# Behind the loop: the last dh stores and half of K's reload on GpSimd's queue, four repeats on VectorE, two row sums in neighbouring column groups

## The chip, the cores and the metric

The kernel runs on one core of a Trainium2 chip. A core has TensorE (PE, matrix multiplications, with a separate weight load, PEld), VectorE (DVE), ScalarE (ACT), GpSimd (POOL) and SyncE (SP), which work on their own instruction streams in order and wait for one another by semaphores. SP, ACT and POOL also issue DMAs, each on a queue of its own; all transfers are carried out by the core's 16 DMA engines. The metric is the device time of one execution in microseconds (us); lower is better.

## What is computed

The reference is the forward pass and all gradients of a gated mixture of two branches over a sequence u of L = 2048 positions with D = 448 channels:

```
g   = sigmoid((u * gate_w).sum(-1))
a   = causal_conv(u, K) + u * Dskip        # K[d, l]: sum over N = 256 modes of C * exp(dt*A*l) * dt*B, by FFT
b   = relu(u @ w1 + b1)**2 @ w2 + b2       # F = 1792
out = g * a + (1 - g) * b
return out and the gradients of u, A, B, C (real and imaginary), log_dt, Dskip, w1, b1, w2, b2, gate_w
```

Two of the outputs matter below. `out_9`, the gradient of Dskip, is the sum over all positions of g times grad_out times u. `out_14`, the gradient of gate_w, is the sum over all positions of ds times u, where ds is the gradient at the sigmoid's input.

## The kernel before

All activations lie as 128 partitions by 16 slots by 448 channels. The order of the work is written out by hand; every engine executes its instructions in program order.

1. A first stage computes the forward spectra of u and of g times grad_out (`fwd1`, `fwd2`: two steps of an FFT, with a store to a scratch tensor `gd` and a load between them), the gradient of K (`dk_d`), and tables of powers.
2. A loop over 14 groups of 32 channels (`token`, `PERIOD`) builds K by products of tables (`kgen`, `k_out`) and, one group behind, reduces the gradient of K to the modes (`turn_x`, `turn_y`, `back_z`, `back_p`, `back_s`). The dense branch runs between these steps (`D_`, `first_layer`, `second_layer`, `project`): at each "D" of PERIOD a few of its 127 steps are taken, and `done` counts them. `dh` (line 968) computes one block of the hidden gradient on VectorE. Its store to `dhT_d` is not issued at once: it is put on the list `behind`, which `release()` empties at each KO, just after that group's `k_out`.
3. Behind the loop (from line 1159) `release()` is called once more. `rows_in` loads 512 KB rows of the dense branch for the weight gradients, on GpSimd's queue. The weight gradients are cut into units (`units`: `turn` transposes a row, `mul_rows` multiplies, `turn_back` writes out) which `Fl(n)` places between the other work.
4. K is then reloaded from its scratch tensor `k_d` into `xs`, so that it stands as 16 slots of 128 positions: thirteen calls of `reload` and three of `fix` (lines 1273 to 1283), all of them on SP. Positions from 256 on are rounded by the reference's bf16 position index, so many rows of `xs` are copies of others: `again` makes them within SBUF, four on VectorE for partitions 64 to 127 and six on ScalarE for partitions 32 to 63. The skip weight is added to the first row on VectorE, and `fwd1` (line 1430) takes `xs` to K's spectrum, with `fwd2` and the products of spectra behind it. Between the reload and `fwd1` the last channel group's `turn_y`, `back_z`, `turn_x`, `back_p` and `back_s` run, and the first units.
5. The inverse transforms (`inv1`, `inv2`) give the forward output (loop at line 1519) and the gradient of u (loop at line 1570). Between the two loops stand the row sums for `out_9` and `out_14` (line 1563): for each, sixteen matmuls with one weight column, one for each slot, accumulate in one PSUM row, ScalarE copies the row and GpSimd's queue stores it.

The loop's last KO (group 13) comes behind its last "D". By the formula in line 1145 all 127 steps have been taken by then, so `done` equals `total` there. The list `behind` holds four dh stores at that point, blocks 3 to 6 of the last column block, 256 KB each.

Of the kernel before, what the change touches and what calls it, by code (L numbers as in the profile page):

```python
# [19 lines left out]
P = 128  # L20
L, D, N, F = 2048, 448, 256, 1792
LT = L // P
# [306 lines left out]
def kernel(ctx, tc, A_u, A_A_re, A_A_im, A_B_re, A_B_im, A_C_re, A_C_im, A_log_dt, A_Dskip,  # L329
# [3 lines left out]
    nc = tc.nc  # L333
    V, S, G_, T_ = nc.vector, nc.scalar, nc.gpsimd, nc.tensor
# [5 lines left out]
    def dscr(name, n, dt=bf16):  # L340
        return nc.dram_tensor(name, (n,), dt, kind="Internal")
# [5 lines left out]
    k_d = dscr("k_d", VROW * D)  # L347
# [4 lines left out]
    dhT_d = dscr("dhT_d", F * L)  # L352
# [5 lines left out]
    K = Ker(tc, pool, psum)  # L358
# [43 lines left out]
    o = 0  # L402
# [34 lines left out]
    g_b = const.tile([P, LT], bf16, name="g_b")  # L437
# [43 lines left out]
    ps = K.ps("X", [P, FT + 4], bf16)  # L481
# [58 lines left out]
    ps = K.ps("S", [P, 512])  # L540
# [149 lines left out]
    behind = []  # L690

    def release():

        while behind:
            behind.pop(0)()
# [171 lines left out]
    def later(f):  # L867
        lates.append(f)
        if len(lates) > LAG:
            lates.pop(0)()  # L870
# [81 lines left out]
    def second_layer():  # L952

        load_r(7)
        for lb in range(4):
            dblk = dbl[lb % 2].rearrange("p (a l) -> p a l", a=DT)
            for jp in range(HP):
                i = HP * lb + jp
                pss = [bank(), bank()]
                for k in range(2):  # L960
                    for dt in range(DT - 1):
                        T_.matmul(pss[k][:], lhsT=w2Tw[:, jp, dt, k], rhs=dblk[:, dt], start=(dt == 0), stop=False, skip_group_check=True)  # L962
                for k in range(2):
                    h = slice(64 * k, 64 * k + 64)
                    T_.matmul(pss[k][:], lhsT=w2Tw[h, jp, 3, k], rhs=dblk[h, 3], start=False, stop=True, tile_position=(64 * k, 0), skip_group_check=True)  # L965
                for k in range(2):
                    S.mul(hblk[:, 2 * jp + k], pss[k][:], 2.0)  # L967
                def dh(i=i, jp=jp, lb=lb):
                    hb = hblk[:, 2 * jp:2 * jp + 2]
                    V.tensor_tensor(out=hb.rearrange("p k l -> p (k l)"), in0=hb.rearrange("p k l -> p (k l)"), in1=rr[i % 8], op=ALU.mult)  # L970
                    behind.append(lambda: nc.sync.dma_start(pair_rows(dhT_d, jp, lb), hb))
                    if i + 8 < 4 * HP:
                        behind.append(lambda: load_r(i + 8, nc.sync))
                later(dh)
                yield
            if lb < 2:
                behind.append(lambda lb=lb: load_db(lb + 2, nc.sync))
            yield from project(lb, 1, w1T)
# [56 lines left out]
    for k, (x8, g, e, gr) in enumerate(ekeys):  # L1035
        T_.matmul(tiles[e][32 * gr:32 * gr + 32, 0:D], lhsT=ct["Ew"][:, 32 * k:32 * k + 32], rhs=hss[x8 // 2][:, g, x8 % 2, :], start=(k == first[e, gr]), stop=(k == last[e, gr]),
                  tile_position=(0, 32 * gr), skip_group_check=True)
    stA, stB = (K.t("st", [P, 4, D], bufs=2) for i in range(2))
    for e in range(6):
        st_ = (stA if e < 4 else stB)[:, e % 4]  # L1040
        if e == 5:
            st_ = st_[0:1]
# [97 lines left out]
    for c in range(1, NCH):  # L1140
        k = 0
# [15 lines left out]
                for g in range(NG):  # L1157
                    nc.sync.dma_start(flat(Gts[0][32 * g:32 * g + 32]), tl(G2, g))
    D_(total)
    release()  # L1160
    Gt = Gts[0]
    DB2 = KW[:, NA * D:].rearrange("p (t d) -> p t d", d=D)

# [85 lines left out]
    def Fl(n=1):  # L1249
        nonlocal nf  # L1250
        for _ in range(n):
            next(fill, None)
            nf += 1

    Fx = K.t("F17", [P, 8704])
    xs = Fx[:, 0:7168].rearrange("p (t d) -> p t d", d=D)
# [3 lines left out]
    xq = 0  # L1260

    def reload(p0, n, j, m, row, *dims):

        nonlocal xq
        xq += 1
        nc.sync.dma_start(xs[p0:p0 + n, j:j + m].rearrange("p m d -> p (m d)"), bass.AP(tensor=k_d, offset=row * D, ap=[[x * D, y] for x, y in dims] + [[1, m * D]]))

    def fix(p0, step, n, j, row, st_):

        nonlocal xq  # L1270
        xq += 1
        nc.sync.dma_start(xs[p0:p0 + step * (n - 1) + 1:step, j], bass.AP(tensor=k_d, offset=row * D, ap=[[st_ * D, n], [1, D]]))
    reload(64, 64, 0, 2, 32, (2, 4), (48, 16))
    reload(64, 64, 3, 1, 48 + 32, (2, 4), (48, 16))
    reload(32, 32, 0, 4, 8, (4, 2), (48, 16))
    reload(32, 32, 7, 1, 48 + 8, (4, 2), (48, 16))
    for j, m, row in ((0, 4, 0), (4, 4, 16), (8, 8, 24)):
# [3 lines left out]
    fix(79, 16, 4, 3, 34, 2)  # L1281
    fix(47, 16, 2, 7, 12, 20)
    fix(31, 1, 1, 15, 8, 1)

    def again(p0, cp, j, m, i, step=1, rep_=1):

        dst = xs[p0:(2 * p0), j:j + 1]
        src = xs[p0:2 * p0, i:i + 1]
        cp(run(dst[:, 0, 0:1], 0, [step * D, rep_], [D, m], [1, D]), run(src[:, 0, 0:1], 0, [0, rep_], [D if step == 1 else 0, m], [1, D]))
# [28 lines left out]
    again(64, V.tensor_copy, 5, 2, 1, 4, 3)  # L1318
    again(64, V.tensor_copy, 7, 1, 3, 4, 3)
    for j, m, i in ((8, 4, 0), (4, 2, 0), (6, 1, 1), (12, 2, 2), (14, 1, 1), (15, 1, 7)):  # L1320
        again(32, S.copy, j, m, i)
    got = {32: [0, 1, 2, 3, 0, 1, 1, 7, 0, 1, 2, 3, 2, 3, 1, 7], 64: [0, 1, 0, 3, 0, 1, 1, 3] + [0, 1, 1, 3] * 2}
    for p0, w in ((32, {0: 0, 8: 1, 4: 2, 12: 3, 16: 7}), (64, {0: 0, 8: 1, 16: 3})):
        assert [w[int(vp[p0, j]) - LT * p0] for j in JO] == got[p0]
# [92 lines left out]
    rc = K.t("rec", [P, RS])  # L1417
# [56 lines left out]
    for q in range(4):  # L1474
# [5 lines left out]
        if q == 1:  # L1480
# [4 lines left out]
            Uv = U[:, :, 0:D]  # L1485
# [23 lines left out]
    Fl(2)  # L1509

    dgt = rc[:, 0:256].rearrange("p (k m) -> p k m", k=2)
    row = rc[0:1, 512:512 + 2 * D].rearrange("p (k d) -> p k d", k=2)
    dg = const.tile([P, LT], fp32, name="dg")
    gp = const.tile([P, LT], bf16, name="gp")
    V.tensor_tensor(out=gp[:], in0=g_b[:], in1=omg_b[:], op=ALU.mult)
# [1 line left out]
    ds_b = const.tile([P, LT], bf16, name="ds_b")  # L1517
    ds32 = const.tile([P, LT], fp32, name="ds32")
    for q in range(4):
# [4 lines left out]
        for x in range(2):  # L1524
            pp = K.pair()
            K.inv2(hs, q, x, pp, [[(negI, brq[q][:, hp, x])] for hp in range(2)])
            for hp in range(2):
                t = 2 * q + x + 8 * hp
                ps = pp[hp][:, 0:D]
# [22 lines left out]
    GU = GU_[:, 0:7168].rearrange("p (t d) -> p t d", d=D)  # L1552
# [7 lines left out]
    pgs = (None for dt in range(2, 4) for _ in param_grads(dt))  # L1560
    hsn = load_hs(2, 0)
    Fl(4)
    for k, (lw, rw, o_) in enumerate(((g_b, GU, out_9), (ds_b, Uv, out_14))):
        ps = K.ps("N%d" % k, [P, 512])
        for t in range(LT):
            T_.matmul(ps[0:1, 0:D], lhsT=lw[:, t:t + 1], rhs=rw[:, t, :], start=(t == 0), stop=(t == LT - 1))  # L1566
        S.copy(row[:, k], ps[0:1, 0:D])
        G_.dma_start(o_.rearrange("(o d) -> o d", o=1), row[:, k])
    Fl(5)
    for q in range(4):  # L1570
        hs = hsn
# [3 lines left out]
        for x in range(2):  # L1575
            ps = K.pair()
            l0l = 2 * q + x
            for hp in range(2):
                t = l0l + 8 * hp
# [17 lines left out]
    ps = K.ps("N1", [P, P], bf16)  # L1597
# [6 lines left out]
    ps = K.ps("X", [P, P], bf16)  # L1604
# [34 lines left out]
```

## Time and profile before

| | us |
|---|---|
| median of three runs | 816.03 |
| lowest, highest | 811.8, 819.44 |
| the profiled execution's own time | 817.63 |
| its span, first to last instruction | 815.8 |

| engine | busy us | share of the span | instructions |
|---|---|---|---|
| PE | 621.9 | 76% | 6749 |
| PEld | 299.4 | 37% | 6749 |
| DVE | 625.3 | 77% | 983 |
| ACT | 506.0 | 62% | 831 |
| POOL | 163.9 | 20% | 264 |

The mean granted TensorE clock is 0.86 of full speed. A row of the profile names the line of the kernel (L1266), the engine (SPq and the like are the engine's own issuing of DMAs), the operation, and the tiles as "written<-read". A name in brackets with an arrow is what ended the idle time before it. Times in the timeline count from the span's start. DMA share is the mean busy share of the 16 DMA engines.

### The profile page before, as it was taken

The page shows a single profiled execution, that of the slowest core. Times are in us where ns is not written, and L with a number is a line of the kernel's source. Part 1 is how long each engine was busy: PE and PEld are TensorE (multiplying, and loading weights), DVE is VectorE, ACT ScalarE, POOL GpSimd, SP SyncE. Part 2 cuts the span into 40 slices and gives each one's busy share as a digit, 9 for nine tenths or more (in the row PEclk, how much of TensorE's full clock was granted, in tenths as well). Part 3 has the DMA queues.
Part 4 walks back from the last instruction along what each step waited for, and adds up shares of the span by engine and source line. Part 5 has one row for each costly group of instructions (what it writes and reads, how often), then busy time and mean ns, then how long its engine had stood idle before and what let it go on. Part 6 is the DMA issues. An engine that isn't in the chain of part 4 may idle for free. (4 is left out here: it accounts for less than half of the span.)

```text
span 815.8 us, 16878 instructions
## 1 busy us (share of the span) xinstructions
PE 621.9 (76%) x6749; PEld 299.4 (37%) x6749; DVE 625.3 (77%) x983; ACT 506.0 (62%) x831; POOL 163.9 (20%) x264
## 2 busy tenths in 40 slices
PE   3676467653378889898978978898778788899985
PEld 1222222121234344344534443444534333444442
DVE  3795597877826999999889999998656974687353
ACT  0696567670577676677866766673675577264553
POOL 1222000042111222222321011101034311023112
PEclk9965655575689999899989999999989799799998
DMA  9978866278758577978696979996689998899972
GB/s 193 237 200 279 302 244 231 90 291 208 209 115 180 114 179 167 174 157 191 190 187 119 288 190 251 181 263 162 212 311 324 343 314 282 260 281 330 261 196 64
DMA packets 179694, 178.87 MB, mean 219 GB/s; under 512 B 116549, under 2 KB 157471, under 8 KB 179023
## 3 DMA queue, kind: packets, MB, share of 16 engines
q1 hardware_dynamic: 152632, 101.04, 50.7%
q0 software_dynamic: 17552, 56.44, 22.6%
q10 hardware_dynamic: 9430, 20.31, 7.1%
q8 instruction: 53, 0.87, 0.4%
q14 instruction: 27, 0.21, 0.1%
HBM read 83.67 MB, written 67.53 MB: 185 GB/s over the span
## 5 line engine op out<-in xcount | busy, mean ns | idle before, releaser
L816 ACT CAST P<-psF 128x1024 bf16<-128x1024 f32 x56 | 57.0, 1018 | 36.5 <-PE psF L814 35.9
L656 DVE TENSOR_TENSOR F<-X,F 128x1024 bf16<-128x1024 bf16 (+2 forms) x42 | 64.4, 1533 | 4.1 <-ACT F L711 2.4
L882 PEld LDWEIGHTS <-U 128*128 128x128 bf16 x448 | 40.0, 100 | 52.9 <-issue 15.0
L882 PE MATMUL psN<-D,U 128*128 128x448 bf16 x224 | 52.6, 372 | 6.3 <-DMA D<-in_B_w_dram 3.6
L1196 PEld LDWEIGHTS <-S 128*128 128x128 bf16 x416 | 40.2, 101 | 40.9 <-issue 13.7
L887 POOL DMA_DIRECT2D br_d<-D x32 | 17.9, 560 | 182.7 <-ACT D L886 176.2
L814 PE MATMUL psF<-R,S 41*32 41x256 bf16 x896 | 24.4, 288 | 37.0 <-DVE P L827 16.8
L1196 PE MATMUL psX<-D,S 128*128 128x449 bf16 x224 | 49.4, 365 | 1.5 <-ACT S L1202 1.5
L882 PE MATMUL psN<-S,U 128*128 128x448 bf16 x224 | 48.0, 358 | 2.5 <-DVE U L970 2.4
L826 DVE TENSOR_TENSOR M<-P,psF 128x2048 bf16<-128x2048 bf16 x28 | 34.0, 1215 | 17.1 <-PE psF L772 17.1
L1196 PE MATMUL psX<-K,S 128*128 128x448 bf16 x192 | 43.7, 374 | 1.8 <-ACT S L1199 1.8
L962 PE MATMUL psN<-S,K 128*128 128x512 bf16 x168 | 44.4, 404 | 0.0
L1187 ACT ACTIVATE S<-psN 128x1024 bf16<-128x1024 bf16 x32 | 33.0, 1030 | 14.9 <-PE psN L1183 14.8
L904 PE MATMUL psN<-S,K 128*128 128x512 bf16 x168 | 42.2, 388 | 0.0
L967 ACT ACTIVATE U<-psN 128x512 bf16<-128x512 f32 x56 | 30.8, 605 | 15.5 <-PE psN L965 11.4
L303 PE MATMUL psN<-D,cb_MI 64*128 64x448 bf16 x96 | 31.7, 514 | 9.0 <-DVE D L288 5.7
L886 ACT CAST D<-psN 128x448 bf16<-128x448 f32 x32 | 17.0, 532 | 33.7 <-PE psN L882 33.7
L657 DVE TENSOR_TENSOR X<-F 128x512 bf16<-128x512 bf16 (+2 forms) x42 | 35.6, 849 | 1.4
L772 PE MATMUL psF<-ident,X 128*128 128x128 bf16 x448 | 33.1, 232 | 4.0 <-ACT P L816 3.9
L303 PEld LDWEIGHTS <-cb_MI 64*128 64x128 bf16 x256 | 17.0, 105 | 51.9 <-issue 46.5
L265 PEld LDWEIGHTS <-M 128*64 128x64 bf16 x192 | 13.8, 133 | 60.1 <-issue 53.6
L827 DVE TENSOR_TENSOR P<-P,psF 128x2048 bf16<-128x2048 bf16 x28 | 34.2, 1221 | 1.0
(346 smaller groups left out, 1596.6 us busy)
## 6 DMA issues: line engine op xcount, KB each, us to landing
sp<-K ACTq DMA_DIRECT2D x8, 896.0 KB
dhT_d<-U SPq DMA_DIRECT2D x28, 256.0 KB
R<-sp SPq DMA_DIRECT2D x8, 896.0 KB
S<-dhT_d POOLq DMA_DIRECT2D x14, 512.0 KB, 6.8
R<-hd SPq DMA_DIRECT2D x16, 448.0 KB
S<-rT_d POOLq DMA_DIRECT2D x12, 512.0 KB, 7.0
hd<-st SPq DMA_DIRECT2D x13, 448.0 KB
rec<-rec_d POOLq DMA_DIRECT2D x11, 448.0 KB, 4.6
```

Source lines behind the costliest of these rows:

```text
L303: nc.tensor.matmul(ps[kk2][:, 0:D], lhsT=MI[r0:r0 + 64, m, :], rhs=rh[r0:r0 + 64], start=(k_ == 0), stop=(k_ == len(terms) - 1), tile_posi ...
L656: V.tensor_tensor(out=Vt[:, 0:2 * w * n], in0=run(lo, 0, [0, 2], [NA, w], [1, n]), in1=run(PX[:, 0:1], 512 * k, [2, w], [0, n], [1, 2]), o ...
L657: V.tensor_tensor(out=run(lo, n, [NA * X2, 2], [NA, X2], [1, n]), in0=run(vb, 0, [n * X2, 2], [n, X2], [1, n]), in1=run(vb, (w + X2) * n, ...
L772: T_.transpose(ps[:, t, 128 * b:128 * b + 128], Xs[c % 2][:, o_:o_ + 128], ident[:])
L816: S.copy(zbs[c, g // 2][:, :, g % 2].rearrange("p t h k n -> p t k h n"), psz[:].rearrange("p t (k h n) -> p t k h n", k=2, h=2))
L826: V.tensor_tensor(out=pr.rearrange("p t g h k n -> p t (g h k n)"), in0=zv, in1=xv, op=ALU.mult)
L827: V.tensor_tensor(out=zv, in0=zv, in1=rev_dim(xv, 1), op=ALU.mult)
L882: T_.matmul(ps[:, 0:D], lhsT=hblk[:, j, P * tt:P * tt + P], rhs=ws[:, j, :], start=(w == 1 and j == 0), stop=(j == FT - 1))
L904: T_.matmul(pss[k][:], lhsT=w1w[:, dt, j * P:j * P + P], rhs=UT[:, dt, 512 * lb:512 * lb + 512], start=(dt == 0), stop=False, skip_group_c ...
L962: T_.matmul(pss[k][:], lhsT=w2Tw[:, jp, dt, k], rhs=dblk[:, dt], start=(dt == 0), stop=False, skip_group_check=True)
L1187: S.activation(hn(i)[:, 8 * th:8 * th + 8, :], ps[:], ACT.Square if i < FT else ACT.Copy)
L1196: T_.matmul(ps[:, 0:w], lhsT=hn(i)[:, t, :], rhs=(DB2[:, t, :] if i < FT else U[:, t, 0:w]), start=(t == 0), stop=(t == LT - 1))
```

## The change

- The dh stores take POOL's queue when all dense steps are done at the time they are issued, else SP's as before.
- The extra `release()` moves from ahead of the units to behind K's reload. (By the order above, the release in the last KO has emptied the list before either place.)
- The sixteen loads of K's reload alternate between POOL's and SP's queue, beginning with POOL: eight each.
- Of the six copies for partitions 32 to 63, the first two (four slots and two slots) stay on ScalarE; the other four (one, two, one and one slots) go to VectorE.
- The two row sums are interleaved slot by slot. They write rows 0 and 32 of one PSUM bank from column groups 0 and 32 of TensorE; the two copies and stores follow behind both.

```diff
-                    behind.append(lambda: nc.sync.dma_start(pair_rows(dhT_d, jp, lb), hb))
+                    behind.append(lambda: (G_ if done >= total else nc.sync).dma_start(pair_rows(dhT_d, jp, lb), hb))
...
     D_(total)
-    release()
     Gt = Gts[0]
...
     def reload(p0, n, j, m, row, *dims):
         nonlocal xq
         xq += 1
-        nc.sync.dma_start(xs[p0:p0 + n, j:j + m].rearrange("p m d -> p (m d)"), ...)
+        (nc.sync, G_)[xq % 2].dma_start(xs[p0:p0 + n, j:j + m].rearrange("p m d -> p (m d)"), ...)
     def fix(p0, step, n, j, row, st_):
         nonlocal xq
         xq += 1
-        nc.sync.dma_start(xs[p0:p0 + step * (n - 1) + 1:step, j], ...)
+        (nc.sync, G_)[xq % 2].dma_start(xs[p0:p0 + step * (n - 1) + 1:step, j], ...)
...
     fix(31, 1, 1, 15, 8, 1)
+    release()
...
     for j, m, i in ((8, 4, 0), (4, 2, 0), (6, 1, 1), (12, 2, 2), (14, 1, 1), (15, 1, 7)):
-        again(32, S.copy, j, m, i)
+        again(32, S.copy if j in (8, 4) else V.tensor_copy, j, m, i)
...
-    for k, (lw, rw, o_) in enumerate(((g_b, GU, out_9), (ds_b, Uv, out_14))):
-        ps = K.ps("N%d" % k, [P, 512])
-        for t in range(LT):
-            T_.matmul(ps[0:1, 0:D], lhsT=lw[:, t:t + 1], rhs=rw[:, t, :], start=(t == 0), stop=(t == LT - 1))
-        S.copy(row[:, k], ps[0:1, 0:D])
-        G_.dma_start(o_.rearrange("(o d) -> o d", o=1), row[:, k])
+    ps = K.ps("N0", [P, 512])
+    for t in range(LT):
+        for k, (lw, rw) in enumerate(((g_b, GU), (ds_b, Uv))):
+            T_.matmul(ps[32 * k:32 * k + 1, 0:D], lhsT=lw[:, t:t + 1], rhs=rw[:, t, :], start=(t == 0), stop=(t == LT - 1),
+                      tile_position=(0, 32 * k), skip_group_check=True)
+    for k, o_ in enumerate((out_9, out_14)):
+        S.copy(rc[32 * k:32 * k + 1, 512:512 + D], ps[32 * k:32 * k + 1, 0:D])
+        G_.dma_start(o_.rearrange("(o d) -> o d", o=1), rc[32 * k:32 * k + 1, 512:512 + D])
```

More of the change, by code (lines that the diff above doesn't have):

```diff
@@ L1265, in reload @@
         xq += 1
-        nc.sync.dma_start(xs[p0:p0 + n, j:j + m].rearrange("p m d -> p (m d)"), bass.AP(tensor=k_d, offset=row * D, ap=[[x * D, y] for x, y in dims] + [[1, m * D]]))
+        (nc.sync, G_)[xq % 2].dma_start(xs[p0:p0 + n, j:j + m].rearrange("p m d -> p (m d)"), bass.AP(tensor=k_d, offset=row * D, ap=[[x * D, y] for x, y in dims] + [[1, m * D]]))
     def fix(p0, step, n, j, row, st_):
@@ L1271, in fix @@
         xq += 1
-        nc.sync.dma_start(xs[p0:p0 + step * (n - 1) + 1:step, j], bass.AP(tensor=k_d, offset=row * D, ap=[[st_ * D, n], [1, D]]))
+        (nc.sync, G_)[xq % 2].dma_start(xs[p0:p0 + step * (n - 1) + 1:step, j], bass.AP(tensor=k_d, offset=row * D, ap=[[st_ * D, n], [1, D]]))
     reload(64, 64, 0, 2, 32, (2, 4), (48, 16))
@@ L1511 @@
     dgt = rc[:, 0:256].rearrange("p (k m) -> p k m", k=2)
-    row = rc[0:1, 512:512 + 2 * D].rearrange("p (k d) -> p k d", k=2)
     dg = const.tile([P, LT], fp32, name="dg")
```

## The prediction

> **What bounds the kernel now.** The change touches two places, the 30 us behind the loop (570 to 601 us of the span) and two row sums at 753 us. So I read the stretches around them first (time from:to, length, busy time of PE, weight loads, DVE, ACT, POOL with instructions, granted clock, DMA share, GB/s).
>
> ```profile
> 584.00:594.50 10.50, 6.15 (x69) 3.94 (x67) 5.26 (x8) 7.17 (x9) 0.00 (x0) 0.99 0.34 93
> 594.50:622.50 28.00, 25.32 (x161) 13.94 (x161) 20.84 (x48) 18.59 (x29) 13.88 (x24) 0.88 0.98 328
> 757.50:760.50 3.00, 3.00 (x17) 1.27 (x15) 0.00 (x0) 0.61 (x2) 0.49 (x2) 1.00 0.49 131
> 760.00:785.00 25.00, 22.17 (x173) 11.34 (x172) 11.17 (x28) 14.56 (x35) 6.54 (x12) 0.94 1.01 286
> 785.00:816.00 31.00, 20.34 (x157) 10.55 (x155) 14.25 (x39) 13.00 (x32) 5.73 (x11) 0.89 0.29 74
> ```
>
> From 584 to 594.5 neither PE (6.15 of 10.5 us) nor the DMA engines (0.34) are full: something else holds the kernel. From 594.5 on both are nearly full. Next, the orders of the two queues and who SP waited for in 569 to 625 us (total, times, longest):
>
> ```profile
> 570.39 0.90 SPq L763 DMA_DIRECT2D k_d<-P  x2
> 571.39 6.19 SPq L971 DMA_DIRECT2D dhT_d<-U  x4
> 578.40 12.28 SPq L1266 DMA_DIRECT2D F<-k_d  x13
> 590.72 1.66 SPq L1272 DMA_DIRECT2D F<-k_d  x3
> 592.50 0.35 SPq L383 DMA_DIRECT2D M<-c_M  x1
> ```
> ```profile
> SPq L255 <- DMA gd<-D: 5.5, 2, 4.1
> ...
> SPq L1266 <- DMA dhT_d<-U: 3.8, 4, 2.3
> ...
> SPq L1266 <- DMA k_d<-P: 0.5, 1, 0.5
> ```
>
> K goes out at 570.39 and the first reload starts at 578.40, having waited 0.5 us for K's store: that start is K's landing, not the dh stores' issue. But the sixteen reloads then take until 592.4, held four times for the landing of a dh store (3.8 us). Now the engines that need the reload:
>
> ```profile
> 584.66 1.03 ACT L1187 ACTIVATE R<-psN 128x1024 bf16<-128x1024 bf16 x1
> 588.99 4.84 ACT L1289 COPY F<-F 32x1792 bf16<-32x1792 bf16 x6 [3.31 <-DMA F<-k_d]
> ...
> 595.25 0.55 ACT L1199 CAST S<-psX 128x448 bf16<-128x448 f32 x1
> ```
> ```profile
> 588.48 1.81 DVE L1289 COPY F<-F 64x448 bf16<-64x448 bf16 x3
> 592.54 0.62 DVE L1289 COPY F<-F 64x1344 bf16<-64x1344 bf16 x1 [2.25 <-DMA F<-k_d]
> 593.19 0.38 DVE L1326 TENSOR_TENSOR F<-F,dsk_bc 1x448 bf16<-1x448 bf16 x1
> ```
> ```profile
> 579.30 1.65 PE L1183 MATMUL psN<-ident,X 128*128 128x128 bf16 x16 [0.35 <-DMA X<-rT_d]
> ...
> 588.85 0.27 PE L843 MATMUL psS<-P,cb_sel 128*32 128x256 bf16 x1
> 589.05 1.69 PE L1196 MATMUL psX<-K,R 128*128 128x448 bf16 x8
> ...
> 595.85 3.15 PE L1196 MATMUL psX<-K,R 128*128 128x448 bf16 x8 [4.66 <-ACT S L1199]
> 598.79 0.95 PE L244 MATMUL psN<-F,cb_F1BD 128*128 128x448 bf16 x2
> ...
> 601.10 0.54 PE L244 MATMUL psN<-F,cb_F1BD 128*128 128x448 bf16 x2
> ```
>
> This is the knot. ACT waits 3.31 us for the reload, then copies for 4.84 us, and only then reaches the evacuation L1199 that PE needs to go on: PE stands 4.66 us, and its next eight matmuls take 3.15 us where eight took 1.69. `fwd1` starts at 598.79.
>
> **The change, part by part.**
>
> *The dh stores.* `done` equals `total` at the last "D" ahead of the last KO, so the release in that KO empties the list in both kernels and the moved `release()` finds nothing. What changes is the queue: the four stores leave SP and go to POOL, ahead of `rows_in(0)` and `rows_in(1)`; the reloads are issued behind them. What is known of such rows and stores on POOL (the two issues in the timeline; issues in 569 to 574 us, KB each, median us to landing; the same form of store earlier on, busy and mean ns):
>
> ```profile
> 570.85 1.07 POOL L1178 DMA_DIRECT2D X<-rT_d  x2
> ```
> ```profile
> X<-rT_d POOLq DMA_DIRECT2D x2, 512.0 KB, 8.8
> S<-rT_d POOLq DMA_DIRECT2D x2, 512.0 KB, 10.9
> ```
> ```profile
> L912 POOL DMA_DIRECT2D rT_d<-S x14 | 10.8, 773 | 39.1 <-ACT S L911 39.1
> ```
>
> Four issues at 0.77 are 3.1 us of POOL in front of the rows, and four times 256 KB on its queue. That is as many bytes as rows 0 and 1 put ahead of rows 2 and 3. Those are issued 1.07 us later and need 10.9 us against 8.8, so they land some 3.2 us behind 0 and 1. So row 0, for which PE waits at 579.30, would land 0 to 3.2 us later; I take 2.0, since the dh stores then no longer run on SP's queue beside it. Behind that turn stands ACT's evacuation, then X's last turn, DVE's products and its copies: all 2.0 later.
>
> *The reload.* SP's eight issues wait for no dh store any more. The last three of before, which nothing held, took 1.66 us, 0.55 each, so eight are out by about 583. POOL's eight wait for K's landing at 578.4 as well and cost between 0.53 (half of 1.07) and 0.77 each, 583 to 585; the last two may be held until rows 0 and 1 have landed, which is no later. Queued behind them on POOL are `rows_in(2)`, `rows_in(3)` and the s_d store. Row 2 goes out near 584 instead of 572; PE asks for it right behind the matmuls of 589.05, at 590.7 + 2.0, and with the DMA engines at 0.34 it should be there in less than the 8.8 quoted. If the last reload took 7.75 us to land, as a load does below with DMA full, it would be there at 592 to 593, while DVE's chain of copies, which cannot start before 588.48 + 2.0 = 590.5, is under way. So the reload ceases to be the last wait; if that cover were gone, each microsecond would cost one.
>
> *The repeats.* By shape (mean ns of one):
>
> ```profile
> L1289 ACT COPY F<-F 32x896 bf16<-32x896 bf16 x2 | 1.9, 932 | 0.0
> ...
> L1289 ACT COPY F<-F 32x1792 bf16<-32x1792 bf16 x1 | 1.7, 1684 | 3.3 <-DMA F<-k_d 3.3
> ...
> L1289 DVE COPY F<-F 64x1344 bf16<-64x1344 bf16 x2 | 1.2, 620 | 2.2 <-DMA F<-k_d 2.2
> ...
> L1289 DVE COPY F<-F 64x448 bf16<-64x448 bf16 x1 | 0.3, 275 | 0.0
> ```
>
> ACT keeps 1.68 + 0.93 = 2.6 us of copies, from 585.7 without the wait, and is through at 588.3 (590.3 with the 2.0). L1199 then comes when its matmuls end (589.05 + 1.69 = 590.7), not at 595.25: PE's next matmuls start at 595.85 - 4.5 = 591.3, or 593.3 with the 2.0. DVE gains three copies at 0.275 and one of 896, which I put at 0.45 between its rows: 1.3 us. Its chain is 588.5 + 1.8 + 0.6 + 1.3 + 0.4 = 592.6, or 594.6. PE's eight matmuls end at 593.3 + 1.7 = 595.0. The two meet: `fwd1` starts at about 595.0, 3.8 us earlier. The clock adds some: the eight matmuls go at 1.69 instead of 3.15 (within the 3.8), and the first two pairs at 0.54 instead of 0.95, 0.8 us more. PE is thus 4.6 us ahead; without the delay of row 0 it would be 6.6, and with 3.2 of it 3.4.
>
> *What is late next.* 1 MB of M2 and the other loads wait on SP not for the reload any more but for the last L843, which frees their buffers: 588.85 + 0.27 + 2.0 = 591.1 instead of 592.5, only 1.4 earlier. From 594.5 to 622.5 the DMA engines are 0.98 busy, and at the end SP waits up to 4.1 us for the gd stores before it may load the spectrum. If DMA decides, the gain is 1.4 plus the free 2% of 28 us (0.6): 2.0. If PE decides, 4.6. I take 3.2, a little below the middle, as the row says full.
>
> *The row sums.* Two matmuls of the loop's sums in different column groups, PE's row sums and L323 behind them, SP's loads for it, and a step of the chain that ended last:
>
> ```profile
> 569.39 0.28 PE L843 MATMUL psS<-M,cb_sel 128*32 128x256 bf16 x1
> 569.39 0.28 PE L843 MATMUL psS<-P,cb_sel 128*32 128x256 bf16 x1
> ```
> ```profile
> 753.23 3.19 PE L1566 MATMUL psN<-K,g_b 128*1 128x448 bf16 x16 [0.67 <-DVE K L1553]
> ...
> 766.48 0.38 PE L323 MATMUL psN<-R,cb_Etw 64*32 64x448 bf16 x8
> ...
> 781.54 0.38 PE L323 MATMUL psN<-R,cb_Etw 64*32 64x448 bf16 x7 [1.33 <-DMA R<-hd]
> ```
> ```profile
> 759.14 2.37 SPq L312 DMA_DIRECT2D R<-hd  x4
> ```
> ```profile
> 773.75 7.75 DMA R<-hd
> ```
>
> Matmuls in different column groups start at the same instant (569.39, 569.39), so the two sums of sixteen matmuls run side by side, and one 3.19 us chain, less its tail, is saved: 3.0 us off PE. But PE would then reach L323 at 763.5, and what it reads was asked for at 759.14 by SP, whose time does not hang on the sums. The next such load takes 7.75 us (PE waits 1.33 us for it at 781.54), and DMA is full (1.01) from 760 to 785. Only the dip of 757.5 to 760.5 (0.49, so 1.5 us free) can be used. The bounds are 0 and 3.0; I take 0.7.
>
> **Sum.** 3.2 + 0.7 = 3.9 us from the profiled execution's 817.63, which gives 813.7. The median of the runs is 816.03, 1.6 below that execution, and the forecast is against it: **812**.
>
> **Rivals.**
>
> *A, nothing absorbs it* (chance 0.25). The gd stores keep pace with `fwd1` and the load for L323 lands early. 4.6 + 3.0 = 7.6 with row 0's delay, 6.6 + 3.0 = 9.6 without: 806.4 to 808.4, say 807. For it: from 785 on DMA is at 0.29, and PE sets the end. Against: the two shares of 0.98 and 1.01.
>
> *B, the rows are late* (chance 0.13), on the other side. POOL's queue carries the dh stores first. If their 1 KB pieces crawl beside K's small ones, row 0 lands later than the 3.2 allow. At 2 us the SP loads are 1.4 ahead, so they are level at 3.4, and `fwd1` is level at 2.0 + 4.6 = 6.6. At a delay of 8 us PE is 1.4 and SP 4.6 behind; less 0.7 of the sums that is 1 to 4 slower, 818.5 in the middle. Against it: the same bytes ahead of rows 2 and 3 cost 3.2.
>
> *C, the queue is no remedy* (chance 0.15). Reloads, dh stores and rows share the same DMA engines, so two queues save issue time only. Eight issues at 0.55 are 4.4 us: the last reload issues at 588 instead of 592.4 and lands so much earlier; less the 2.0 of row 0 that leaves `fwd1` 2.4, of which by the shares above half survives: 1.2 + 0.7, time 814. The Trainium skill states this ("DMA: Bandwidth & Descriptors", section "Issuing engines are not separate DMA queues": several issuing engines interleave on the same 16 engines and save only the sequencer's time). The trace speaks against this rule at this place, since 3.8 us of SP's waits there are for landings of dh stores, not issue.
>
> **Chances and range.** Forecast 0.47, A 0.25, C 0.15, B 0.13. One per cent, about what a measurement here tells from no change, is 8.2 us. Only A reaches it, and then not surely, so faster by over 1% has 0.22, mostly A's. Slower by over 1% needs more than B's price: 0.05. Within 1%: 0.73. The three runs shown lie from 811.8 to 819.44, so the range goes from A's 806 less a little to B's 818.5: 805 to 819.
>
> **What would show it.** Right: SP's reloads end near 583 and ACT's wait before L1289 is gone; PE's 4.66 us wait for L1199 is under 1 us and the matmuls behind it take 1.7; `fwd1` starts near 595; the last gd landing is 2 to 4 us earlier; the row sums span 3.2 us and a new wait of 1 to 3 us for R<-hd stands before L323. Wrong: PE's wait for X<-rT_d over 4 us (B); PE without a wait at L323 (A); SP's reloads held for dh landings as before, ending near 588 (C).

## The result: 0.6% slower, and the profile after

The changed kernel takes 819.96 us in the median of 20 runs (812.73 to 828.29), the kernel before 816.41 us in 20 runs on the same chip (809.95 to 821.65). The ratio is **1.0061, with a 95% interval of 1.0036 to 1.0086**: some 5.0 us slower (0.0061 of 816.4), between 2.9 and 7.0. The forecast was 812.0 with a range of 805 to 819: the sign was wrong, and the median lies 1 us outside the range.

The profiled execution is one of the slower ones (825.01 us), and in it K's store (SPq L763, `k_d<-P`) comes at 573.91 where it came at 570.39 before, though nothing ahead of it was changed. So **times below that carry a plus count from K's store** of the same profile. M2 is the 1 MB load M<-c_M (SPq L383), and the spectrum's load is the first K<-gd (SPq L255).

The two queues behind the loop in the changed kernel, from the timeline (start, length, queue, line, operation, number; in brackets the idle time before it and what ended it), SP first, then POOL:

```profile
573.91 0.90 SPq L763 DMA_DIRECT2D k_d<-P  x2
581.23 4.29 SPq L1265 DMA_DIRECT2D F<-k_d  x6
593.22 2.07 SPq L1271 DMA_DIRECT2D F<-k_d  x2
599.72 0.34 SPq L383 DMA_DIRECT2D M<-c_M  x1
```
```profile
574.38 2.84 POOL L971 DMA_DIRECT2D dhT_d<-U  x4
577.22 1.11 POOL L1177 DMA_DIRECT2D X<-rT_d  x2
581.53 2.81 POOL L1265 DMA_DIRECT2D F<-k_d  x5 [3.20 <-DVE K L1292]
585.42 0.49 POOL L1265 DMA_DIRECT2D F<-k_d  x1 [1.09 <-DMA dhT_d<-U]
588.87 0.49 POOL L1265 DMA_DIRECT2D F<-k_d  x1 [2.95 <-DMA X<-rT_d]
593.16 0.51 POOL L1271 DMA_DIRECT2D F<-k_d  x1 [3.81 <-DMA F<-k_d]
593.67 1.11 POOL L1177 DMA_DIRECT2D S<-rT_d  x2
```

The rows X go out at +3.31 instead of +0.46: the four dh stores take POOL 2.84 us. The dh stores were taken off SP's queue so that they no longer hold the reload. Now POOL's half of it is held for a dh store (1.09), for a row (2.95) and for other reloads (3.81). SP's waits in the same stretch (total, times, longest) show the rest:

```profile
SPq L1271 <- DMA F<-k_d: 9.0, 2, 7.7
...
SPq L383 <- DVE M L826: 2.3, 1, 2.3
SPq L383 <- PE psS L843: 2.1, 1, 2.1
```

SP's two repairs (`fix`) wait 9.0 us for reloads, so the reload is out at 595.29, +21.4, where it was at +22.0 before. But M2 no longer waits for that: it waits for the engines. PE's timeline tells for what they wait:

```profile
588.64 1.89 PE L1182 MATMUL psN<-ident,X 128*128 128x128 bf16 x16 [6.40 <-DMA X<-rT_d]
...
599.41 0.27 PE L843 MATMUL psS<-P,cb_sel 128*32 128x256 bf16 x1
...
601.92 1.67 PE L1195 MATMUL psX<-K,R 128*128 128x448 bf16 x8 [0.17 <-ACT S L1198]
603.43 0.54 PE L244 MATMUL psN<-F,cb_F1BD 128*128 128x448 bf16 x2
```

**PE stands 6.40 us for row 0**, which is turned at +14.73 instead of +8.91. The last L843 is over at 599.68 and M2 goes out at 599.72, +25.8 instead of +22.1. The knot of before is gone (the wait of 4.66 us for ACT's evacuation is 0.17, the eight matmuls take 1.67 instead of 3.15), and from row 0 to `fwd1` there are 14.8 us instead of 19.5; all of that is eaten by the 5.8 us of row 0, and `fwd1` starts at +29.5 instead of +28.4. M2's lateness stays: the spectrum's load goes out at +56.7 instead of +52.2 (SP's timeline, before and after):

```profile
622.54 0.34 SPq L255 DMA_DIRECT2D K<-gd  x1
```
```profile
630.63 0.33 SPq L255 DMA_DIRECT2D K<-gd  x1
```

The other place, from the timeline of the changed kernel: PE's row sums (the first two; they run until 760.3) and the L323 behind them, then POOL's row load and SP's hd load:

```profile
757.12 0.35 PE L1565 MATMUL psN<-K,g_b 128*1 128x448 bf16 x1 [0.67 <-DVE K L1552]
757.12 0.35 PE L1565 MATMUL psN<-D,ds_b 128*1 128x448 bf16 x1
...
770.18 0.35 PE L323 MATMUL psN<-R,cb_Etw 64*32 64x448 bf16 x1 [2.77 <-DMA R<-hd]
772.18 0.57 PE L323 MATMUL psN<-R,cb_Etw 64*32 64x448 bf16 x7 [1.66 <-DMA R<-hd]
```
```profile
763.13 0.56 POOL L1177 DMA_DIRECT2D S<-dhT_d  x1 [0.92 <-PE psN L1182]
```
```profile
763.72 2.37 SPq L312 DMA_DIRECT2D R<-hd  x4
```

The two sums do start together, and 3.0 us are off PE. But PE then waits 4.4 us in two parts for hd where it waited for nothing before, and L323 starts 13.1 us behind the first sum, against 13.2 (766.48 less 753.23). In the kernel before, POOL's row load came 3.1 us behind SP's hd load (the hd load at 759.14, quoted above):

```profile
762.26 0.54 POOL L1178 DMA_DIRECT2D S<-dhT_d  x1 [1.47 <-PE psN L1183]
```

Now it goes out 0.59 us ahead of it: the row load hangs on PE, which is 3 us earlier, and the hd load stands on SP behind other loads, which are not.

### The profile page after: what moved, and what is told of

Same layout as the page of the kernel before. It is cut to its first block, busy times and chain, and to the rows that moved or that the text cites. A ratio compares the mean times of both kernels' runs of the same rounds, so it can differ in the third digit from the quotient of the medians.

```text
span 823.2 us, 16879 instructions
## 1 busy us (share of the span) xinstructions
PE 621.3 (75%) x6749; PEld 298.6 (36%) x6749; DVE 626.8 (76%) x987; ACT 504.2 (61%) x827; POOL 170.7 (21%) x276
## 5 line engine op out<-in xcount | busy, mean ns | idle before, releaser
L882 PEld LDWEIGHTS <-U 128*128 128x128 bf16 x448 | 40.4, 101 | 51.1 <-issue 13.7
L882 PE MATMUL psN<-D,U 128*128 128x448 bf16 x224 | 53.1, 374 | 2.4 <-DVE U L914 1.5
L962 PE MATMUL psN<-S,K 128*128 128x512 bf16 x168 | 46.4, 418 | 0.1
L904 PE MATMUL psN<-S,K 128*128 128x512 bf16 x168 | 43.1, 395 | 0.0
L1195 PE MATMUL psX<-K,S 128*128 128x448 bf16 x192 | 40.9, 356 | 2.0 <-ACT S L1198 2.0
L1186 ACT ACTIVATE S<-psN 128x1024 bf16<-128x1024 bf16 x32 | 32.9, 1030 | 14.1 <-PE psN L1182 14.0
L265 PEld LDWEIGHTS <-M 128*64 128x64 bf16 x192 | 14.6, 138 | 62.6 <-issue 57.9
L795 ACT COPY S<-K 128x128 bf16<-128x128 bf16 x56 | 34.6, 1002 | 0.0
```

What stands on the lines that cost most here:

```text
L795: S.copy(D2[:, :, 0, 4 * l:4 * l + 4].rearrange("p (g i) a -> p a g i", g=NG), DK[:, l::4].rearrange("p a (e g q i) -> p a e q g i", g=NG, ...
L882: T_.matmul(ps[:, 0:D], lhsT=hblk[:, j, P * tt:P * tt + P], rhs=ws[:, j, :], start=(w == 1 and j == 0), stop=(j == FT - 1))
L904: T_.matmul(pss[k][:], lhsT=w1w[:, dt, j * P:j * P + P], rhs=UT[:, dt, 512 * lb:512 * lb + 512], start=(dt == 0), stop=False, skip_group_c ...
L1186: S.activation(hn(i)[:, 8 * th:8 * th + 8, :], ps[:], ACT.Square if i < FT else ACT.Copy)
L1195: T_.matmul(ps[:, 0:w], lhsT=hn(i)[:, t, :], rhs=(DB2[:, t, :] if i < FT else U[:, t, 0:w]), start=(t == 0), stop=(t == LT - 1))
```

## The experiments

Theories: **R**, the loss is row 0, late behind the dh stores on POOL's queue. **S**, it is made at the row sums. **Q**, it is made by the reload on two queues. In the later expectations: **L**, it is what GpSimd's half of the reload waits for, and who waits for that; S1 and S2, the sums lose by the order of the hd load and the row load, or by full DMA engines whatever the order; D and E, the stretch after M2 is set by the transfers, or by PE and the evacuations. Ratios are to the kernel before in runs on the same chip; its medians were 815.15 us (e1 to e4), 814.32 (e5 to e8), 814.23 (e9 to e12) and 815.29 (e13 to e16), 35 runs each against 12 of each kernel.

### e1: the dh stores alone

Before, with:

```diff
-  behind.append(lambda: nc.sync.dma_start(pair_rows(dhT_d, jp, lb), hb))
+  behind.append(lambda: (G_ if done >= total else nc.sync).dma_start(pair_rows(dhT_d, jp, lb), hb))
```

> The kernel before with one edit: the last four dh stores on POOL's queue. Theory R (the stores stand on POOL ahead of the row loads and hold row 0): PE waits 5 to 7 us for row 0 where it waited 0.35, the copies on ScalarE lose their wait for the reload, and the time is 2 to 5 us longer. Theory S (the loss is made at the row sums): no change beyond 1 us. Theory Q (the loss is made by the reload on two queues): no change beyond 1 us.

Measured: 815.46 us, ratio 1.0002 (0.9969 to 1.0035). PE's and SP's timelines:

```profile
584.86 1.89 PE L1183 MATMUL psN<-ident,X 128*128 128x128 bf16 x16 [4.55 <-DMA X<-rT_d]
```
```profile
571.76 0.88 SPq L763 DMA_DIRECT2D k_d<-P  x2
579.27 15.47 SPq L1266 DMA_DIRECT2D F<-k_d  x13
...
596.55 0.35 SPq L383 DMA_DIRECT2D M<-c_M  x1
```

Row 0 is late by 4.2 us (+13.1), and M2 by 2.7 (+24.8). A loss of 2.7 us would be 0.33%, at the interval's upper end: the dh stores alone are no measurable loss, nor any gain. PE's wait for row 0 came nearly as R had it (4.55 us where it said 5 to 7); the 2 to 5 us of time did not.

### e2: the row sums alone

Before, with the sums as in the change.

> The kernel before with one edit: the two row sums side by side. Theory S: the 3 us saved on PE come back whole or more as a wait for the load of hd in front of L323 (4 us as in the changed kernel, none before), so the time is 0 to 3 us longer. Theories R and Q: the sums are as forecast, 0.7 us shorter (0 to 3), with a wait of 1 to 3 us at L323.

Measured: 817.86 us, ratio 1.0025 (0.9995 to 1.0054), by itself just inconclusive. PE's, SP's and POOL's timelines show the changed kernel's order and its wait (the other seven matmuls of this L323 wait another 1.60):

```profile
760.57 0.53 PE L323 MATMUL psN<-R,cb_Etw 64*32 64x448 bf16 x1 [2.90 <-DMA R<-hd]
```
```profile
754.25 2.38 SPq L312 DMA_DIRECT2D R<-hd  x4
```
```profile
753.39 0.54 POOL L1178 DMA_DIRECT2D S<-dhT_d  x1 [0.92 <-PE psN L1183]
```

### e3: the change without its dh stores on POOL

```diff
-  behind.append(lambda: (G_ if done >= total else nc.sync).dma_start(pair_rows(dhT_d, jp, lb), hb))
+  behind.append(lambda: nc.sync.dma_start(pair_rows(dhT_d, jp, lb), hb))
```

> The changed kernel with one edit undone: the last dh stores on SP's queue again, as before in front of the reload. Theory R: row 0 lands in time (PE waits under 1 us for it), fwd1 starts 3 to 6 us earlier after K's store than the changed kernel's 29.5 us, and the time is 3 to 6 us below the changed kernel, 812 to 815 beside 816 to 817 of before. Theory Q: the loss stays, 818 to 820. Theory S: about 819.

Measured: 815.46 us, ratio 0.9999 (0.9971 to 1.0027). The loss is gone: row 0 at +9.6, the reload out at +17.8, M2 at +20.4, `fwd1` at +24.1, the spectrum's load at +49.3. The queue of the dh stores is what turns the change into a loss, though by itself (e1) it costs nothing that can be measured.

### e4: the dh stores on SP, behind the reload

The split reload and the repeats as in the change, the sums one after the other, and

```diff
                 if c < NCH - 1:
                     YTs[c] = [load_yt(c, g) for g in range(NG)]
-                release()
+                    release()
```

so that the last dh stores wait for the `release()` behind the reload and leave on SP.

> The reload on two queues and the repeats shared as in the changed kernel, the dh stores on SP really behind the reload (the release in the last KO is left out, the one behind the reload empties the list), the row sums one behind the other as before. Theory R: rows and reload both land early, fwd1 starts 23 to 25 us after K's store (28.4 before), and the time is 3 to 6 us below before. Theory Q: no faster than before. Theory S: 3 to 5 us below the changed kernel, from the sums alone.

Measured: 815.86 us, ratio 1.0002 (0.9971 to 1.0033). The reload is out at +15.6, M2 at +19.2 and `fwd1` at +23.0, the earliest so far; but the spectrum's load goes out at +52.1. From M2 to it there are 32.9 us, where before has 30.0 and e3 28.9. Perhaps the 1 MB of dh stores, which then runs in the stretch in which DMA is full, takes back what was won; it is not shown, as e10, with the stores early, has 32.5. The 3 to 6 us that R gave here were not measured.

### e5 and e6: the hd load ahead of the raw loads

```diff
+    hsn = load_hs(2, 0)
     Dw = K.t("U16", [P, 8192])
...
     pgs = (None for dt in range(2, 4) for _ in param_grads(dt))
-    hsn = load_hs(2, 0)
```

e5 is before with the parallel sums and this edit, e6 is e3 (the change with dh on SP) with it. The first two loads of hd thus go out some 4 us ahead of the sums instead of 6 behind their start.

> The kernel before with the row sums side by side and the first load of hd for the last loop moved ahead of the fourteen loads of raw parameters and sums on SP. Theory S1 (with the sums shorter, the next row load on POOL is issued 0.6 to 0.9 us ahead of the load of hd instead of 3.1 us behind it, and PE then waits 4.5 us for hd): the wait before L323 goes, L323 starts 10 us after the sums' start (13.1 with the wait), and the time is 2 to 4 us below before. Theory S2 (DMA is full behind the sums, so the order changes nothing): the same wait turns up in front of another load, and the time is within 1 us of before.

> The changed kernel with the last dh stores on SP as before, and the first load of hd for the last loop ahead of the raw parameters. Theory S1: 2 to 4 us below the same kernel without the move (815.5), and with the 2 us of the front kept, 4 to 6 below before. Theory S2: 815, as without the move.

Measured: e5 815.43 us, 1.0011 (0.9976 to 1.0045); **e6 809.25 us, 0.9930 (0.9898 to 0.9963)**, faster than both kernels. In both, L323 starts 10.2 us behind the first sum, with no wait for hd in front of it, 3.0 earlier than with the sums in a row. e6 is 0.69% below e3 (0.9930 against 0.9999), more than the 0.25% by which e2 was slower; e5 against e2 (1.0011 against 1.0025) is too close to tell.

### e7: the repeats alone

```diff
-        again(32, S.copy, j, m, i)
+        again(32, S.copy if j in (8, 4) else V.tensor_copy, j, m, i)
```

> The kernel before with one edit: four of the six copies on VectorE. Theory D (behind the reload the DMA engines decide: the load of gd follows the issue of M2's load by 29 to 31 us whatever fwd1 does): fwd1 starts 3 to 5 us earlier after K's store than 28.4, but M2 stays near 22, the load of gd near 52, and the time is within 1 us of before. Theory E (PE and the evacuations decide): the load of gd moves with fwd1, and the time is 3 to 5 us below before.

Measured: 814.63 us, ratio 0.9987 (0.9954 to 1.0021). PE's and SP's timelines:

```profile
595.52 0.54 PE L244 MATMUL psN<-F,cb_F1BD 128*128 128x448 bf16 x2
```
```profile
570.58 0.88 SPq L763 DMA_DIRECT2D k_d<-P  x2
...
592.63 0.35 SPq L383 DMA_DIRECT2D M<-c_M  x1
...
623.67 0.33 SPq L255 DMA_DIRECT2D K<-gd  x1
```

`fwd1` comes 3.5 us earlier (+24.9), M2 where it was (+22.1), and the spectrum's load is not earlier at all (+53.1 against +52.2). **PE's gain in this place is worth nothing that can be measured as long as M2 goes out no earlier.** (An earlier M2 is not always a gain either: e4 and e11 have it at +19.2 and the time of before.)

### e8: the split reload alone

```diff
-        nc.sync.dma_start(xs[p0:p0 + n, j:j + m]...
+        (nc.sync, G_)[xq % 2].dma_start(xs[p0:p0 + n, j:j + m]...
```

and the same in `fix`.

> The kernel before with one edit: the reload on SP and POOL in turn. Theory D: M2's load is issued near 20 after K's store instead of 22, the load of gd comes 2 us earlier (50) though fwd1 keeps its six copies on ScalarE and starts at 25 to 27, and the time is 1 to 2 us below before. Theory E: the load of gd moves only as far as fwd1 does.

Measured: 810.73 us, ratio 0.9953 (0.9925 to 0.9982). Q falls: the split is the one part that gains by itself. The reload is out at +19.1, M2 goes at +21.0. SP, which still carries the dh stores, waits 1.5 us for their landings instead of 3.8, and 4.4 for reloads instead of 2.9:

```profile
SPq L1272 <- DMA F<-k_d: 4.4, 1, 4.4
...
SPq L1272 <- DMA dhT_d<-U: 0.8, 2, 0.5
...
SPq L1266 <- DMA dhT_d<-U: 0.7, 2, 0.4
```

### e9: the change without its row sums

The sums one after the other as in before, all else as changed.

> The changed kernel with the two row sums one after the other again; the dh stores on GpSimd, the split reload and the repeats stay. Theory R+S (the loss of 0.6% is the sum of what the dh stores on GpSimd do to the rows, about 2.5 us, and of what the parallel sums do at the hd load, about 2.5 us): ratio 1.002 to 1.005, and the stretch from the row sums to the end is 56.5 to 58 us instead of 59.5. If the rows alone make the loss: ratio 1.005 to 1.008 as with the sums. If the sums alone make it: 0.994 to 0.999. All three expect the landmarks behind K's store as in the changed kernel: the first row turned at +14 to +15 us, M2 asked for at +25 to +26, K's gd load at +56 to +57.

Measured: 819.70 us, ratio 1.0053 (1.0016 to 1.0089). Most of the loss stays, so S is not the whole; the interval is too wide to size the sums by this run. Together with e1 (1.0002), e7 (0.9987) and e8 (0.9953) it shows that the parts do not add: with the dh stores on POOL the split's gain is gone, and more. PE's and POOL's timelines:

```profile
583.87 1.89 PE L1182 MATMUL psN<-ident,X 128*128 128x128 bf16 x16 [5.22 <-DMA X<-rT_d]
```
```profile
759.25 0.56 POOL L1177 DMA_DIRECT2D S<-dhT_d  x1 [1.48 <-PE psN L1182]
```

Row 0 is late again (+13.7), and the row load is back 2.3 us behind the hd load (756.94), without a wait at L323.

### e10: rows 2 and 3 ahead of the reload

```diff
-    rows_in(0)
-    rows_in(1)
+    for r_ in range(4):
+        rows_in(r_)
```

and no `rows_in(2)`, `rows_in(3)` further down.

> The changed kernel with all four row loads of the turn issued by GpSimd behind the dh stores and ahead of the reload, as in the kernel before, where rows 2 and 3 follow the first turn. Theory R1 (rows 2 and 3, held behind GpSimd's reloads to +19.8 us, are what makes the stage from M2's load on later): the second turn waits less, M2 is asked for at +22 to +24 instead of +25.8, the gd load at +53 to +55, time 1 to 3 us below the changed kernel, ratio 1.002 to 1.005. Theory R2 (the first row's delay alone, +5.8 us, makes it): first row at +14 to +16, M2 at +25 to +26, ratio 1.005 to 1.008. If GpSimd's reloads, now behind 1 MB more of rows, take the place of the wait: reload out at +25 or later, fwd1 at +30 or later, ratio 1.006 or more.

Measured: 819.09 us, ratio 1.0064 (1.0035 to 1.0094). Row 0 is at +12.3, M2 at +23.1, the spectrum's load at +55.7. M2 is earlier than in the changed kernel and the loss is the same: that rows 2 and 3 are held behind POOL's reload is not the cause.

### e11 and e12: the dh stores earlier, on SP

```diff
             if c == NCH - 1 and o == "S0":
+                release()
```

The four stores then leave on SP ahead of K's store. e11 is before with this alone; e12 is e6 with it.

> The kernel before with the last dh stores given to SyncE ahead of K's store instead of behind it; nothing of the change. Theory H (what holds the reload in the kernel before is that it queues behind the dh stores' landings, 3.8 us of waits, whichever engine issues it): no wait of the reload for a dh landing, the reload out by +19 instead of +22, M2 at +19 to +20.5, time 1 to 4 us below the kernel before, ratio 0.995 to 0.999. Theory Q (it is the issue time of one queue, so that only a second queue helps): reload out at +21 to +22, M2 at +22, ratio 0.999 to 1.002. If K's store is late behind the dh stores, all landmarks keep their distance from it and K itself is 1 to 3 us later: ratio 1.001 to 1.004.

> The changed kernel with the last dh stores on SyncE ahead of K's store, and the hd load ahead of the loads of the raw input: the split reload, the repeats and the parallel sums stay. If the early dh stores add to what the version with dh on SyncE and the hd load ahead gave (ratio 0.993): 0.988 to 0.992, reload out at +16 to +18. If that version had it all: 0.991 to 0.995. If the early dh stores make K's store later: 0.994 to 0.998.

Measured: e11 814.23 us, 0.9986 (0.9959 to 1.0013); e12 812.03 us, 0.9953 (0.9922 to 0.9983). In e11 one queue has the reload out at +19.0, as two queues have in e8 (+19.1): before, the landings of the dh stores held it, not the issuing alone. (Taking the stores off SP is not enough: in e1 the reload is out at +24.7, held 8.7 us for landings of its own loads.) The profiles show M2 at +19.2 and +18.7; the time of e11 does not show a gain beyond its interval, and e12 is no better than e6.

### e13: the first rows ahead of the dh stores

The closest test of row 0: the changed kernel, with POOL's order turned round.

```diff
                     YTs[c] = [load_yt(c, g) for g in range(NG)]
-                release()
+                    release()
...
     rows_in(0)
     rows_in(1)
+    release()
```

> The changed kernel with the first two row loads ahead of the dh stores on GpSimd, which still carries the stores, half the reload and rows 2 and 3 behind them. Theory R (the first rows' delay of 5.8 us makes the loss): first row turned at +8.5 to +10 us behind K's store instead of +14.7, gd load at +51 to +54, ratio 0.997 to 1.001 (the parallel sums' price is left). Theory L (GpSimd's half of the reload, which waits for landings of dh stores and rows, and what waits for it make the loss): first row early all the same, reload out at +19 to +22 as in the changed kernel, M2 at +23 or later, ratio 1.003 to 1.007.

Measured: 815.53 us, ratio 0.9987 (0.9948 to 1.0025): **the loss is gone**, with the dh stores still on POOL, and POOL's half of the reload behind them. POOL's, PE's and SP's timelines:

```profile
574.38 1.08 POOL L1177 DMA_DIRECT2D X<-rT_d  x2
575.44 2.87 POOL L971 DMA_DIRECT2D dhT_d<-U  x4
...
757.03 0.54 POOL L1177 DMA_DIRECT2D S<-dhT_d  x1 [0.92 <-PE psN L1182]
```
```profile
583.94 1.89 PE L1182 MATMUL psN<-ident,X 128*128 128x128 bf16 x16 [2.25 <-DMA X<-rT_d]
...
761.62 0.35 PE L323 MATMUL psN<-R,cb_Etw 64*32 64x448 bf16 x1 [0.30 <-DMA R<-hd]
763.67 0.38 PE L323 MATMUL psN<-R,cb_Etw 64*32 64x448 bf16 x7 [1.70 <-DMA R<-hd]
```
```profile
756.22 2.41 SPq L312 DMA_DIRECT2D R<-hd  x4
```

Row 0 at +10.0, the reload out at +18.7, M2 at +20.9, `fwd1` at +24.6, the spectrum's load at +50.8. In this profile SP also happened to reach the hd load 0.8 us ahead of POOL's row load, and PE waits 0.30 and 1.70 us at L323 instead of 2.77 and 1.66. So the two places are not kept apart here: whether the other executions of this kernel had the hd load first too is not known.

### e14: the repairs on the queue of the reload that they overwrite

```diff
-        (nc.sync, G_)[xq % 2].dma_start(xs[p0:p0 + step * (n - 1) + 1:step, j]...
+        (G_ if p0 == 31 else nc.sync).dma_start(xs[p0:p0 + step * (n - 1) + 1:step, j]...
```

> The changed kernel with each of the three single-row repairs of the reload issued on the queue whose reload it overwrites, so that SyncE has no wait of 9.0 us for GpSimd's reload; the dh stores stay ahead of the rows on GpSimd. Theory L: SyncE's part of the reload is out by +14 instead of +21.4, the repeats start earlier, fwd1 at +26 to +28, ratio 1.000 to 1.004. Theory R: the first row stays at +13 to +15, the turn and M2 with it (+24 to +26), ratio 1.004 to 1.008.

Measured: 818.56 us, ratio 1.0052 (1.0022 to 1.0081). SP's waits:

```profile
SPq L1271 <- DMA F<-k_d: 5.8, 1, 5.8
...
SPq L383 <- DVE M L826: 4.5, 1, 4.5
SPq L383 <- PE psS L843: 2.1, 1, 2.1
```

SP's part of the reload is out at +17.3 instead of +21.4 (POOL's, and so all of it, at +18.9, as early as in e13), and the time does not move: row 0 is at +12.8, and SP's gain goes over into M2's own wait for the engines (M2 at +23.8). SP's 9.0 us were not on the path. Against e13, on the same chip, this kernel has the reload as early, row 0 2.8 and M2 2.9 us later, and the loss.

### e15 and e16: controls

e15 is before with only the hd load moved; e16 is e6 with the edit of e14.

> The kernel before with nothing but the hd load for the last quarter moved ahead of the loads of the raw input. If the order of the loads is worth something by itself: the wait of 1.3 us for hd behind the first group goes, ratio 0.996 to 0.999. If it only mends what the parallel sums spoil: ratio 0.999 to 1.002.

> The version with the dh stores on SyncE and the hd load ahead (0.993), with the three repairs on the queues whose reloads they overwrite. In that version SyncE waits 5.2 us and GpSimd 3.0 us for reload landings before the repairs. If that wait is on the path: reload out at +14 to +16 instead of +18.7, M2 up to 1 us earlier, ratio 0.990 to 0.993. If the turn and its row 2 decide instead: landmarks from M2 on within 1 us, ratio 0.992 to 0.996.

Measured: e15 814.61 us, 1.0003 (0.9971 to 1.0035): with the sums in a row, the order of the loads is worth nothing that can be measured, and so e6's gain over e3 is taken to be a mending of what the parallel sums spoil. e16 812.20 us, 0.9969 (0.9934 to 1.0004): the repairs' queue brings no gain here either.

### The landmarks together

Means of the profiles, from K's store, of three kinds: the dh stores ahead of row 0 on POOL (e1, e9, e10, e14); one queue for the reload and row 0 early (before, e2, e5, e7, e15); two queues and row 0 early (e3, e4, e6, e8, e12, e13). The changed kernel's own profile, e11's and e16's are in none of them.

| | row 0 | M2 | spectrum's load |
|---|---|---|---|
| dh ahead of row 0 | +13.0 | +23.8 | +54.0 |
| one queue, row 0 early | +8.7 | +22.0 | +52.7 |
| two queues, row 0 early | +9.4 | +20.0 | +49.9 |

And from the first row sum to the end: 56.4 us with the sums in a row (before, e1, e4, e7, e8, e9, e11), 59.4 with parallel sums and the row load ahead of the hd load (e2, e3, e10, e14; L323 waits 3.9 to 5.1 us in all), 54.9 with parallel sums and the hd load ahead (e5, e6, e12, e13; no wait, in e13 2.0).

## Why the prediction was wrong

**Row 0** was the step that failed first. The term was 2.0 us with bounds of 0 and 3.2; the changed kernel's profile has 5.8, the four others 3.3 to 4.8. The bound came from rows 2 and 3 behind rows 0 and 1: 1.07 us for the issue of two row loads and 2.1 of later landing. Four stores take longer to issue; the 3.1 us for that stood in the text and were not put in. In the changed kernel they are 2.84, and the landing takes 11.4 us behind its issue (577.22 to 588.64) instead of 8.4, another 3.0: 5.8.

**The reload** was to be out by 583 to 585 (+12.6 to +14.6); it was out at +21.4. That POOL's last two loads would be held for rows 0 and 1 was said, but as no delay. Missed were that POOL's loads would also wait for the dh stores, from which SP's were freed, and that SP's repairs would wait 9.0 us for reloads. e14 shows no measurable price for these 9.0 us; row 0 was later still.

**The repeats and PE's knot** came as worked out: the wait at L1199 gone, 1.67 us for the eight matmuls, and 4.7 us less from row 0 to `fwd1`, where the terms gave 5.8.

**What is late next** was named rightly, M2 behind the last L843, with the right point of balance: in before the last L843 is over 3.4 us ahead of M2's load (589.12 and 592.50), so a delay of it under 3.4 costs M2 nothing and one over it costs the excess. With 2.0 that was a gain of 1.4. In the changed kernel's profile the 5.8 of row 0 have grown to 7.0 at the last L843 (PE was slower there, see the last section), and M2 is 3.7 late; in the mean of the four others it is 1.8 late. The half share for PE was wrong: e7 gives PE 3.5 us and the time nothing that can be measured, as the row with 0.98 had said.

**The row sums** had the size right (3.0 us off PE) and the sign of the net wrong: 0.7 us gained was the term, and e2 has 2.0 lost (0.25% of 815; interval from 0.4 gained to 4.4 lost). SP's time does not hang on the sums, as the text says; but the landing does. The row load behind the sums, which comes 3 us earlier with them, was not followed, and it passes the hd load. That this order makes the wait at L323 is shown by e5 and e6, where it is gone.

**Sum.** M2 1.8 to 3.7 late and the sums 2.0: 3.8 to 5.7 us, against 5.0 (2.9 to 7.0) measured, and against a gain of 3.9 forecast. That these meet is in part luck: e9, without the parallel sums, is still 4.3 us slower (1.3 to 7.2). **Rival B** was the mechanism, "the rows are late", with its sign (PE's wait for X<-rT_d over 4 us) and the price of a delay of 8 us for one of 5.8; it had 0.13, since the same bytes ahead of rows 2 and 3 had cost 3.2. **Rival C** fell with its sign and its mark (no reload of SP is held for a dh store in the changed kernel). The rule of the Trainium skill that it names ("DMA: Bandwidth & Descriptors", section "Issuing engines are not separate DMA queues"), that a second issuing engine saves only the sequencer's time, is not refuted by e8's gain of 0.47% (0.18 to 0.75): its reload is out 3 us earlier, and eight issues at 0.55 are 4.4. But time to issue is not all that counts here, since with one queue e11 has the reload out as early, without the waits for the dh stores.

**What is shown and what is open.** That the dh stores on POOL's queue turn the change into a loss is shown by e3, which takes them off it and has no loss, though its profile has the full wait at L323 (4.7 us). That it is their place ahead of the rows is made likely by e13, which has no loss, with e10 and e14, which have it; but e13 and e14 also differ in the order of the hd load and the row load. Up to the first row sum their profiles are 0.4 us apart, from it to the end 5.2. So how the price divides between row 0 and the sums stays open. Nor can the profiles carry M2's lateness to the end: from K's store to the first row sum there are 180.3 us in the mean of the four with the dh stores first, 180.0 with one queue and 176.3 with two, with 5 to 7 us between the kernels of each kind.

Open too: e9 is 1.0% slower than e8 (at least 0.3% by the intervals), about 8 us, and their profiles differ by 2.5 us at M2 and 1.0 at the spectrum's load; but e9's profiled execution took 814.54 us against its median of 819.70. e1 has row 0 and M2 as late as e9 and no loss; its interval allows 2.9 us.

## What to carry to other kernels

When stores are moved to another queue, add both their issue time and their bytes to whatever is issued behind them there, and ask first which of those the bottleneck engine needs next: here the same stores behind two row loads instead of ahead of them were worth 0.7% (e13, with part of it perhaps from the hd load). Where two queues feed one full set of DMA engines, making one engine faster can let its less urgent load pass the urgent one of the other queue; so an edit that speeds up PE needs the order of the loads around it looked at, and the urgent load issued well ahead. The parts of a change do not add up: parts that gained or did nothing by themselves lost together, so time them also one by one.

## What the runs showed of the hardware

- With the row load on POOL's queue ahead of the hd load on SP's by only 0.04 (e14) to 0.86 us (e2), PE waited 3.9 to 5.1 us in all for hd; with 0.8 us the other way round (e13) 2.0, and with the hd load some 10 us ahead (e5, e6) nothing.
- The four 256 KB stores took POOL 2.84 us to issue, 0.71 each. The rows behind them landed in 12.7 us in the median in the changed kernel and in 9.6 to 11.2 in e1, e9, e10 and e14, against 8.8 before and 9.9 in e13 with the rows first (the DMA issues of the changed kernel, 512 KB each):

```profile
X<-rT_d POOLq DMA_DIRECT2D x2, 512.0 KB, 12.7
```

- A queue held its next DMA for the landing of the one eight places ahead of it. In POOL's rows above, behind four stores, two rows and five reloads, the next reload waits for a dh store, the last of the four, and the one behind it for a row, the first of the two; in e10, with four rows behind the four stores, POOL's reloads wait for dh stores, rows X and a row S in turn; and in e8 the four waits of SP for dh stores are those of its last two reloads and its two repairs, eight places behind the four stores. Whether the program or the chip sets this no run shows. This is how stores hold what stands behind them on their queue, and a second queue gives the reload eight more places.
- PE was slower behind a long wait. In all nine profiles in which it waited 1.77 us or more for row 0, the sixteen turns took 1.89 us and the L843 behind them 0.39 to 0.42 each. Behind shorter waits both occur: 1.07 and 0.27 to 0.28 behind 1.08 (e2), 1.89 and 0.39 to 0.42 behind 0.98 (e6). The granted clock over 588.6 to 599.7 in the changed kernel was 0.58, against 0.99 in 584 to 594.5 before (time, length, busy times, clock, DMA share, GB/s):

```profile
588.60:599.70 11.10, 10.36 (x121) 6.97 (x122) 3.31 (x5) 7.86 (x8) 2.10 (x4) 0.58 0.45 137
599.70:630.60 30.90, 28.02 (x197) 15.93 (x198) 26.34 (x61) 20.27 (x30) 14.90 (x26) 1.00 0.96 315
```
